# A new emission list for the first layer of a fused delta-rule and two-MLP kernel, without the idle products behind its first block

## The chip, the cores and the metric

The kernel runs on one core of a Trainium2 chip. Its time is device microseconds of one execution; the kernel before was run three times. The engines are TensorE (PE in the profile, with PEld for its weight loads), VectorE (DVE), ScalarE (ACT), GpSimd (POOL) and SyncE (SP), which issues nearly all DMAs.

## What is computed

Three layers follow one another on 4 batches x 768 positions = 3072 tokens of 8 heads x 48 = 384 values: a delta-rule recurrence, an MLP with squared ReLU (384 to 2048 to 384), and a gated MLP (384 to 1536 to 384).

```python
k_n = k / (np.linalg.norm(k, axis=-1, keepdims=True) + 1e-06)
for t in range(S):
    y[:, :, t] = np.einsum('bhd,bhde->bhe', q[:, :, t], state)
    v_old = np.einsum('bhde,bhd->bhe', state, kt)
    state = state + bt[:, :, :, None] * np.einsum('bhd,bhe->bhde', kt, vt - v_old)
...
h = np.maximum(x @ w_in, 0.0);  x = h * h @ w_out
...
gate = 1.0 / (1.0 + np.exp(-(x @ w_gate)));  out = (gate * (x @ w_val)) @ w_out
```

## The kernel before

**Pieces.** The 768 positions are cut into 12 chunks of 64, two chunks (st 0 and 1) to a group, six groups (g 0 to 5) of 512 tokens. The recurrence becomes matrix algebra in a chunk: scores of the keys with themselves, the inverse of a triangular 64x64 matrix per head, then products that carry a state from chunk to chunk. The MLPs run in fp32 accuracy from rounded pairs: each product is three, high x high, low x high, high x low. All of it, up to the middle of the sixth group's MLP, is emitted by one hand-written list of tokens, `ORDER` (lines 28 to 80); line 760 to 762 walk it, and each token calls a small function that issues a few instructions. The instructions of an engine run in the order in which the list issues them, and SP issues its DMAs in that order too, one after the other: a DMA that waits for its buffer holds up those behind it.

The tokens, with the lines of their instructions:

- Loads: `kn`, `kt`, `kc`, `q`, `v`, `k2`, `kz`, `be` (chunks of keys, queries, values, beta), `f,n` (raw weights of MLP block n, 768 KB, L128).
- Weights of MLP block n = 0 to 15, which arrive as 64-bit floats: `hi` (ACT L134), `b` (DVE L139, L143), `b2` (DVE L148, L152), `lo` (POOL L159), `ch` (ACT L204, the rounded half), `cl` (POOL L208, the rest), `sl` (the rest goes to DRAM as `w1d`, L211); `li,n` and `lw,n` fetch a block's low half back (L644) before each use.
- Recurrence of a chunk: `sq`, `sm`, `no` (norms), `a` (key scores, PE L352, DVE L356), `p` (query scores, PE L381 or L366, mask on DVE L387 or L372), `ti`, `r,g,i`, `to`, `t1` (the inverse on DVE: transposes in L426 and L428, row steps L437 and L441 or L450 and L457, transposes out L467 and L470), `ja`, `jb`, `jc` (groups 0 and 1 only: joining 16-row inverses, PE L482 to L512, ACT L490 to L517), `n`, `w` (joining 32-row inverses, PE L525 and L540, ACT L531 and L544), `ks` (PE L553, DVE L561 and L565), `t` (PE L571, ACT L576), `s` (the state, PE L583, DVE L592), `y` (PE L605 and L607, ACT L610), `z` (rearranging by DMA, L623 to L629), `x` (rounded pair of the MLP's input, ACT L116, DVE L117).
- First MLP, n = 16 g + block: `h,n` (9 matmuls of 128x512, L666, and three ACT passes L680 to L683), `g,n` (the low half of the activation, DVE L689), `o,n` (9 matmuls, L704). `h,n` needs `x` of both chunks and `li,n`; `o,n` needs `g,n` and `lw,n`.
- `w2,i,k`: conversion of the second MLP's weights, in six steps. `po`: a group's result to DRAM.
- `d,k`: k idle products of 128x512 whose result nobody reads (L740).

```python
def keep_warm(n):
    if po[0] is None:
        if not idle:
            nc.gpsimd.memset(zeros, 0.0)
            idle.append(ps_o.tile([128, GT], F32, tag="o2", name="idle"))
        out, x = idle[0], zeros
    else:
        out, x = h_tile(h_next[0]), w1h[0][:, 0:GT]
    for _ in range(n):
        nc.tensor.matmul(out=out, lhsT=x[:, 0:128], rhs=x, start=True, stop=True)
```

**Buffers.** Two chunks at a time fit for each load (`bufs=2`), three PSUM banks for the recurrence (most pieces take two), two for `h`, two `wt` tiles and one `wl` tile for the weight conversion, three slots each for `li`, `lw`, `gh` and `gl`. A tile is given back behind its last use in the list, and one that is asked for early holds its slot until then.

**After the list** the kernel's own loops emit the rest: blocks 82 to 95 of the first MLP in their natural order, and the second MLP (L868 to L945), which is not touched.

Of the kernel before, what the change touches and what calls it, by code (L numbers as in the profile page):

```python
# [33 lines left out]
x,0,0 hi,4 b2,3 ti,1,3 ti,1,1 li,1 sl,2 lo,3 y,0,1 z,0,1 r,1,0 d,1 ch,3 f,6 cl,3 sl,3 lw,0 lw,1 kc,1,0 kc,1,1
s,0,1 r,1,1 x,0,1 v,1,0 li,2 q,1,0 hi,5 b,4 b2,4 lo,4 q,1,1 r,1,2 k2,1,0 b,5 d,2 h,0 li,3 f,7 g,0 h,1 ch,4 b2,5
r,1,3 cl,4 r,1,4 sl,4 d,6 lo,5 kn,2,0 li,4 hi,6 g,1 h,2 f,8 ch,5 cl,5 b,6 lw,2 b2,6 lo,6 sl,5 to,1 kt,2,1 o,0
h,3 t1,1 f,9 lw,3 ch,6 cl,6 li,5 sl,6 hi,7 kn,2,1 b,7 p,1,0 o,1 b2,7 g,2 hi,8 lo,7 ch,7 f,10 lw,4 li,6 cl,7 h,4
sl,7 g,3 v,1,1 ja,1,0 b,8 o,2 lw,5 sv,1,0 ja,1,1 p,1,1 hi,9 b2,8 lo,8 ch,8 li,7 kt,2,0 jb,1,0 f,11 sq,2,0 sq,2,1
cl,8 hi,10 g,4 h,5 jb,1,1 b,9 jc,1,0 jc,1,1 sm,2,0 sl,8 o,3 b2,9 lo,9 g,5 ch,9 cl,9 sl,9 lw,6 li,8 b,10 b2,10
hi,11 h,6 o,4 lw,7 lo,10 f,12 ch,10 cl,10 h,7 li,9 g,6 n,1,0 b,11 o,5 hi,12 b2,11 lo,11 sl,10 ch,11 sv,1,1  # L40
sm,2,1 f,13 cl,11 n,1,1 ks,1,0 b,12 b2,12 sl,11 lw,8 no,2 g,7 h,8 w,1,0 li,10 hi,13 b,13 lo,12 ch,12 cl,12 b2,13
o,6 w,1,1 d,18 sl,12 t,1,0 lw,9 d,4 a,2,0 g,8 lo,13 h,9 f,14 ch,13 cl,13 a,2,1 ti,2 o,7 ti,2,1 h,10 kz,2,0 lw,10
hi,14 g,9 li,11 sl,13 li,12 k2,1,1 y,1,0 z,1,0 b,14 b2,14 lo,14 ti,2,3 o,8 f,15 p,2,0 h,11 kz,2,1 s,1,0 lw,11
r,2,0 ch,14 d,1 d,1 cl,14 sl,14 g,10 g,11 ks,1,1 li,13 r,2,1 o,9 x,1,0 hi,15 lw,12 b,15 li,14 d,5 t,1,1 b2,15
h,12 y,1,1 z,1,1 kn,3,0 lo,15 ch,15 cl,15 p,2,1 g,12 r,2,2 o,10 lw,13 x,1,1 r,2,3 sl,15 h,13 o,11 kn,3,1 lw,14
li,15 kc,2,1 h,14 r,2,4 g,13 r,2,5 o,12 r,2,6 li,16 lw,15 li,17 g,14 d,12 h,15 v,2,0 r,2,7 o,13 h,16 kc,2,0
lw,16 r,2,8 g,15 li,18 q,2,0 o,14 lw,17 r,2,9 r,2,10 s,1,1 li,19 h,17 sq,3,0 kt,3,1 g,16 o,15 po,0 lw,18 g,17
h,18 to,2 t1,2 o,16 sq,3,1 li,20 lw,19 li,21 h,19 g,18 o,17 lw,20 sm,3,1 h,20 q,2,1 sm,3,0 no,3 kt,3,0 g,19
n,2,0 li,22 v,2,1 k2,2,0 n,2,1 o,18 lw,21 sv,2,0 ks,2,0 g,20 h,21 li,23 w,2,0 a,3,0 o,19 w,2,1 lw,22 a,3,1 li,24
kz,3,0 h,22 o,20 g,21 ti,3 t,2,0 g,22 h,23 li,25 sv,2,1 y,2,0 lw,23 ti,3,1 o,21 z,2,0 lw,24 ti,3,3 h,24 li,26  # L50
k2,2,1 g,23 p,3,0 kz,3,1 r,3,0 s,2,0 o,22 ks,2,1 g,24 lw,25 li,27 h,25 o,23 lw,26 r,3,1 g,25 h,26 r,3,2 li,28
o,24 lw,27 t,2,1 g,26 x,2,0 r,3,3 h,27 li,29 y,2,1 kn,4,0 o,25 p,3,1 h,28 lw,28 r,3,4 g,27 li,30 w2,0,0 z,2,1
o,26 lw,29 r,3,5 s,2,1 g,28 li,31 kc,3,0 w2,0,1 h,29 o,27 kn,4,1 li,32 r,3,6 lw,30 g,29 r,3,7 h,30 w2,0,2 x,2,1
o,28 lw,31 r,3,8 w2,0,3 g,30 h,31 li,33 q,3,0 w2,0,4 o,29 lw,32 r,3,9 g,31 h,32 li,34 o,30 kt,4,1 h,33 r,3,10
w2,1,0 g,32 lw,33 to,3 li,35 o,31 w2,0,5 lw,34 t1,3 sq,4,0 g,33 h,34 w2,1,1 li,36 v,3,0 sq,4,1 o,32 po,1 w2,1,2
lw,35 sm,4,0 kt,4,0 w2,1,3 sm,4,1 h,35 g,34 sv,3,0 li,37 kc,3,1 n,3,0 o,33 ks,3,0 lw,36 h,36 g,35 li,38 w2,1,4
v,3,1 no,4 w2,1,5 n,3,1 w,3,0 o,34 lw,37 g,36 w2,2,0 h,37 li,39 k2,3,0 t,3,0 o,35 w,3,1 a,4,0 lw,38 g,37 h,38
a,4,1 li,40 q,3,1 w2,2,1 kz,4,0 o,36 lw,39 y,3,0 ti,4 h,39 k2,3,1 w2,2,2 li,41 sv,3,1 s,3,0 g,38 z,3,0 ti,4,1
w2,2,3 o,37 p,4,0 ti,4,3 lw,40 kz,4,1 g,39 w2,2,4 h,40 r,4,0 li,42 o,38 ks,3,1 lw,41 w2,2,5 li,43 g,40 o,39
w2,3,0 h,41 r,4,1 t,3,1 g,41 h,42 li,44 r,4,2 kn,5,0 o,40 x,3,0 w2,3,1 y,3,1 g,42 h,43 lw,42 lw,43 li,45 w2,3,2  # L60
r,4,3 z,3,1 o,41 lw,44 r,4,4 g,43 w2,3,3 h,44 li,46 r,4,5 kn,5,1 o,42 lw,45 w2,3,4 g,44 h,45 li,47 g,45 p,4,1
o,43 kc,4,0 w2,3,5 r,4,6 w2,4,0 lw,46 x,3,1 h,46 li,48 r,4,7 o,44 lw,47 s,3,1 w2,4,1 sq,5,0 li,49 h,47 g,46
q,4,0 r,4,8 o,45 h,48 w2,4,2 o,46 lw,48 r,4,9 g,47 li,50 h,49 w2,4,3 r,4,10 to,4 lw,49 kt,5,1 g,48 w2,4,4 li,51
v,4,0 o,47 lw,50 w2,4,5 po,2 sv,4,0 t1,4 li,52 h,50 w2,5,0 sm,5,0 kc,4,1 g,49 o,48 sq,5,1 lw,51 q,4,1 sm,5,1
g,50 h,51 li,53 n,4,0 w2,5,1 o,49 ks,4,0 kt,5,0 lw,52 w2,5,2 h,52 li,54 no,5 g,51 v,4,1 n,4,1 w,4,0 g,52 o,50
lw,53 w2,5,3 a,5,1 h,53 w2,5,4 k2,4,0 li,55 w,4,1 a,5,0 o,51 t,4,0 lw,54 kz,5,0 g,53 w2,5,5 k2,4,1 h,54 li,56
li,57 ti,5 o,52 w2,6,0 y,4,0 lw,55 h,55 sv,4,1 z,4,0 ti,5,1 p,5,0 kz,5,1 ti,5,3 d,4 s,4,0 o,53 lw,56 g,54 w2,6,1
h,56 g,55 li,58 r,5,0 o,54 kc,5,0 lw,57 w2,6,2 r,5,1 ks,4,1 g,56 w2,6,3 li,59 h,57 o,55 lw,58 li,60 t,4,1 w2,6,4
g,57 r,5,2 w2,6,5 o,56 h,58 x,4,0 y,4,1 h,59 g,58 w2,7,0 lw,59 p,5,1 li,61 r,5,3 z,4,1 o,57 lw,60 r,5,4 g,59
li,62 w2,7,1 q,5,0 kc,5,1 h,60 o,58 lw,61 w2,7,2 g,60 li,63 h,61 r,5,5 o,59 lw,62 w2,7,3 x,4,1 r,5,6 g,61 h,62  # L70
li,64 w2,7,4 o,60 r,5,7 lw,63 s,4,1 w2,7,5 g,62 li,65 r,5,8 w2,8,0 h,63 o,61 lw,64 g,63 h,64 li,66 r,5,9 o,62
w2,8,1 h,65 lw,65 r,5,10 g,64 li,67 to,5 w2,8,2 o,63 v,5,0 lw,66 po,3 t1,5 g,65 li,68 h,66 n,5,0 sv,5,0 w2,8,3
ks,5,0 o,64 v,5,1 w2,8,4 lw,67 h,67 g,66 li,69 w,5,0 w2,8,5 n,5,1 o,65 q,5,1 t,5,0 lw,68 w2,9,0 w,5,1 g,67 h,68
li,70 o,66 k2,5,1 k2,5,0 lw,69 w2,9,1 g,68 h,69 o,67 li,71 sv,5,1 y,5,0 w2,9,2 lw,70 g,69 h,70 s,5,0 li,72
w2,9,3 o,68 z,5,0 lw,71 g,70 li,73 w2,9,4 ks,5,1 o,69 w2,9,5 lw,72 h,71 g,71 li,74 w2,10,0 o,70 h,72 lw,73 t,5,1
x,5,0 g,72 h,73 li,75 o,71 w2,10,1 lw,74 y,5,1 g,73 h,74 w2,10,2 li,76 o,72 z,5,1 li,77 lw,75 w2,10,3 h,75 o,73
w2,10,4 lw,76 g,74 h,76 w2,10,5 li,78 o,74 lw,77 w2,11,0 g,75 g,76 h,77 li,79 o,75 x,5,1 lw,78 w2,11,1 g,77 h,78
li,80 o,76 w2,11,2 lw,79 g,78 o,77 li,81 li,82 w2,11,3 w2,11,4 h,79 h,80 lw,80 g,79 o,78 o,79 w2,11,5 lw,81 g,80
# [966 lines left out]
```

## Time and profile before

| what | value |
|---|---|
| device time, median of 3 runs | 1121.29 us (1120.75 to 1122.94) |
| profiled execution, first to last instruction (its span) | 1116.7 us |
| PE busy | 1041.1 us, 93% |
| DVE busy | 584.0 us, 52% |
| ACT busy | 428.8 us, 38% |
| POOL busy | 151.4 us, 14% |
| mean granted TensorE clock | 0.972 |

Of the profiled execution only the span is known; the median of the runs is 4.6 us longer, for what lies around the span. The shares are averages over very different stages: the recurrence of group 0 has nothing beside it that PE could do, the middle mixes recurrence and first MLP, and the last 450 us are the second MLP alone.

### The profile page before, as it was taken

The page shows a single profiled execution, that of the slowest core. Times are in us where ns is not written, and L with a number is a line of the kernel's source. Part 1 is how long each engine was busy: PE and PEld are TensorE (multiplying, and loading weights), DVE is VectorE, ACT ScalarE, POOL GpSimd, SP SyncE. Part 2 cuts the span into 40 slices and gives each one's busy share as a digit, 9 for nine tenths or more (in the row PEclk, how much of TensorE's full clock was granted, in tenths as well). Part 3 has the DMA queues.
Part 4 walks back from the last instruction along what each step waited for, and adds up shares of the span by engine and source line. Part 5 has one row for each costly group of instructions (what it writes and reads, how often), then busy time and mean ns, then how long its engine had stood idle before and what let it go on. Part 6 is the DMA issues. An engine that isn't in the chain of part 4 may idle for free.

```text
span 1116.7 us, 27013 instructions
## 1 busy us (share of the span) xinstructions
PE 1041.1 (93%) x11764; PEld 862.7 (77%) x11770; DVE 584.0 (52%) x1099; ACT 428.8 (38%) x688; POOL 151.4 (14%) x117
## 2 busy tenths in 40 slices
...
PEclk9998689899999999999999999999999999999999
...
GB/s 270 125 82 212 250 146 178 164 194 155 129 187 261 204 175 227 157 176 201 167 155 170 164 207 164 45 9 49 1 29 29 0 57 1 16 41 1 29 1 29
DMA packets 93030, 135.56 MB, mean 121 GB/s; under 512 B 45552, under 2 KB 72304, under 8 KB 92400
## 3 DMA queue, kind: packets, MB, share of 16 engines
...
q8 instruction: 92, 1.51, 0.6%
...
HBM read 108.63 MB, written 20.45 MB: 116 GB/s over the span
## 4 chain that ended last, share of the span: by engine, by line
PE 87%; DVE 5%; issue 3%; DMA 2%; POOL 1%; ACT 1%; SPq 0%; DVEq 0%; POOLq 0%
PE gv L868 26%; PE o L704 18%; PE h L666 17%; PE o L894 11%; PE o L930 2%; PE att L583 2%; PE att L540 1%; PE att L525 1%; PE att L571 1%; PE att L605 1%; DMA w1s<-in_w_dram 1%; PE att L553 1%; PE att L352 1%; PE h L740 1%; DVE tt L441 1%
## 5 line engine op out<-in xcount | busy, mean ns | idle before, releaser
L876 DVE TENSOR_TENSOR p<-sg,gv 128x512 f32<-128x512 f32 x72 | 49.5, 688 | 252.6 <-PE gv L868 252.6
L680 ACT ACTIVATE gg<-h 128x512 f32<-128x512 f32 x96 | 57.4, 598 | 195.6 <-PE h L666 186.1
L868 PE MATMUL gv<-xhi,w2h 128*128 128x512 f32 x432 | 121.5, 389 | 0.0
L868 PE MATMUL gv<-xlo,w2h 128*128 128x512 f32 x432 | 121.4, 389 | 0.0
L868 PE MATMUL gv<-xhi,w2l 128*128 128x512 f32 x432 | 121.4, 389 | 0.0
L704 PE MATMUL o<-gh,il 128*128 128x512 f32 x288 | 115.0, 399 | 0.0
L874 ACT ACTIVATE sg<-gv 128x512 f32<-128x512 f32 x72 | 43.2, 600 | 172.5 <-PE gv L868 172.5
L878 ACT CAST ph<-p 128x512 fp32r<-128x512 f32 x72 | 44.8, 622 | 156.5 <-DVE p L876 156.5
L689 DVE TENSOR_TENSOR gl<-gg,gh 128x512 fp32r<-128x512 f32 x96 | 72.1, 755 | 54.2 <-ACT gg L683 54.0
L868 PEld LDWEIGHTS gv<-xhi,w2l 128*128 128x128 f32 x432 | 81.1, 188 | 17.0
L868 PEld LDWEIGHTS gv<-xlo,w2h 128*128 128x128 f32 x432 | 81.1, 188 | 16.9
L868 PEld LDWEIGHTS gv<-xhi,w2h 128*128 128x128 f32 x432 | 81.0, 188 | 16.2
L704 PE MATMUL o<-gl,w1h 128*128 128x512 f32 x216 | 87.2, 404 | 5.0 <-DVE gl L689 4.9
L704 PE MATMUL o<-gh,w1h 128*128 128x512 f32 x216 | 90.6, 419 | 0.0
L666 PE MATMUL h<-xhi,il 128*128 128x512 f32 x288 | 83.1, 397 | 2.2 <-DMA il<-w1d 2.2
L880 DVE TENSOR_TENSOR pl<-p,ph 128x512 fp32r<-128x512 f32 x72 | 50.7, 704 | 49.5 <-ACT ph L878 49.5
L159 POOL TENSOR_TENSOR y<-raw 128x768 f32<-128x768 f32 (+1 forms) x16 | 27.9, 1743 | 314.4 <-DVE raw L152 248.4
L117 POOL TENSOR_TENSOR xlo<-x2r,xhi 128x512 fp32r<-128x512 f32 x18 | 24.7, 1370 | 336.8 <-ACT xhi L116 336.8
L894 PE MATMUL o<-ph,w2h 128*128 128x512 f32 x180 | 70.0, 389 | 0.0
L894 PE MATMUL o<-ph,w2l 128*128 128x512 f32 x180 | 70.0, 389 | 0.0
L894 PE MATMUL o<-pl,w2h 128*128 128x512 f32 x180 | 70.0, 389 | 0.0
L666 PE MATMUL h<-xhi,w1h 128*128 128x512 f32 x216 | 65.7, 413 | 3.5 <-ACT xhi L116 3.5
...
## 6 DMA issues: line engine op xcount, KB each, us to landing
...
```

Of the source, the lines that this page charges most:

```text
L117: eng.tensor_tensor(out=dst_lo, in0=src, in1=dst_hi.bitcast(F32), op=ALU.subtract)
L159: nc.gpsimd.tensor_tensor(out=t, in0=c["t"], in1=c["raw"][:, :, 0].bitcast(F32), op=ALU.add)
L666: nc.tensor.matmul(out=ps[:, cs], lhsT=w[:, kc * 128:kc * 128 + 128], rhs=x[:, kc, cs], start=(i == 0 and kc == 0), stop=(i == 2 and kc == ...
L680: nc.scalar.activation(out=gg, in_=ps, func=ACTF.Relu)
L689: nc.vector.tensor_tensor(out=gl, in0=gg, in1=gh.bitcast(F32), op=ALU.subtract)
L704: nc.tensor.matmul(out=po[m], lhsT=w[:, cs], rhs=x, start=(f == 0 and i == 0), stop=(f == NF1 - 1 and i == 2),)
L868: nc.tensor.matmul(out=ps, lhsT=w[:, kc * 128:kc * 128 + 128], rhs=x[:, kc, :], start=(i == 0 and kc == 0), stop=(i == 2 and kc == KD - 1),)
L874: nc.scalar.activation(out=sg, in_=pss[0], func=ACTF.Sigmoid)
L876: nc.vector.tensor_tensor(out=p, in0=sg, in1=pss[1], op=ALU.mult)
L878: nc.scalar.copy(out=ph, in_=p)
L880: nc.vector.tensor_tensor(out=pl, in0=p, in1=ph.bitcast(F32), op=ALU.subtract)
L894: nc.tensor.matmul(out=po2[m], lhsT=w[:, m * 128:m * 128 + 128], rhs=x, start=(f == 0 and i == 0), stop=(f == NF2 - 1 and i == 2),)
```

## The change

The whole of `ORDER` is written anew. The tokens are the same, each as often as before, but for `d`: eight tokens with 51 idle products (`d,6`, `d,18`, `d,4`, two `d,1`, `d,5`, `d,12`, `d,4`), all behind the first `h`, are gone; the seven single products ahead of it remain. No function, buffer, shape or line outside the list changes. First lines of the list:

```diff
 ORDER = """
-kn,0,1 kn,0,0 kt,0,1 be kt,0,0 sq,0,1 f,1 q,0,0 v,0,1 sq,0,0 v,0,0 f,0 kc,0,0 sm,0,1 f,2 sm,0,0 no,0 kc,0,1 hi,1
...
+kn,0,0 kn,0,1 sq,0,0 sm,0,0 d,1 be sq,0,1 sm,0,1 kt,0,1 cj q,0,0 no,0 kt,0,0 cs d,1 kn,2,0 kc,0,1 a,0,1 v,0,0
...
```

**DVE in the inverse of group 0** (L437 and L441 are row steps, L139 to L152 weight conversion, L387 a mask of `p`, L467 and L470 the transposes out, L314 a norm's sum). Before, from the middle of the row steps:

```order
L437 TENSOR_TENSOR tmp_111<-xi,tt 128x120
L441 TENSOR_TENSOR tt<-tt,tmp_111 128x2x10x6
L148 TENSOR_SCALAR y<-wt 128x768
L152 SCALAR_TENSOR_TENSOR w1s_142<-w1s_142,y 128x768
L139 TENSOR_SCALAR y<-wt 128x768
L143 SCALAR_TENSOR_TENSOR wt<-wt,y 128x768
L387 TENSOR_TENSOR pm<-att,mask 128x512 x2
L437 TENSOR_TENSOR tmp_111<-xi,tt 128x126
L441 TENSOR_TENSOR tt<-tt,tmp_111 128x2x9x7
```

Now the end of the row steps, which run without a break from the first, and what follows:

```order
L437 TENSOR_TENSOR tmp_111<-xi,tt 128x30
L441 TENSOR_TENSOR tt<-tt,tmp_111 128x2x15
L467 STREAM_TRANSPOSE t_107<-tt 128x32x32
L387 TENSOR_TENSOR pm<-att,mask 128x512 x2
L139 TENSOR_SCALAR y<-wt 128x768
L143 SCALAR_TENSOR_TENSOR wt<-wt,y 128x768
L148 TENSOR_SCALAR y<-wt 128x768
L152 SCALAR_TENSOR_TENSOR w1s_283<-w1s_283,y 128x768
L470 STREAM_TRANSPOSE xi<-tt 128x32x32
L314 TENSOR_REDUCE s_445<-kn 128x16
```

The conversion and one mask stood inside the row steps; now they stand between the two transposes out.

**PE between the inverse of group 0 and its first state update** (the second number is the tile's width, x64 is both chunks, x32 one of them; L498 and L512 count 64 and 32 a chunk). Before:

```order
L498 MATMUL att<-join,xi 32x16 x128
L512 MATMUL att<-xi,join 32x16 x64
L525 MATMUL att<-t_107,am 32x32 x64
L540 MATMUL att<-n,xi 32x32 x64
L571 MATMUL att<-v,t_107 64x48 x32
L740 LDWEIGHTS join
L740 MATMUL idle<-join 128x512
L605 MATMUL att<-pm,u_112 64x64 x32
L583 MATMUL att<-u_112,k_114 64x48 x32
```

Now:

```order
L498 MATMUL att<-join,xi 32x16 x64
L512 MATMUL att<-xi,join 32x16 x32
L525 MATMUL att<-t_107,am 32x32 x32
L381 MATMUL att<-q,kc 64x64 x32
L540 MATMUL att<-n,xi 32x32 x32
L571 MATMUL att<-v,t_107 64x48 x32
L498 MATMUL att<-join,xi 32x16 x64
L352 MATMUL att<-kt 64x64 x32
L525 MATMUL att<-t_107,am 32x32 x32
L352 MATMUL att<-kt 64x64 x32
L512 MATMUL att<-xi,join 32x16 x32
L583 MATMUL att<-u_112,k_114 64x48 x32
```

Chunk 0 is joined and multiplied (L571) before the joining of chunk 1 begins, and group 1's key scores (L352) and chunk 0's query scores (L381) stand in the gaps.

**PE in the recurrence of group 1** (L666 and L704 are the first MLP). Before:

```order
L540 MATMUL att<-n,xi 32x32 x32
L740 MATMUL h<-w1h_90 128x512 x18
L571 MATMUL att<-v,t_107 64x48 x32
L740 MATMUL h<-w1h_90 128x512 x4
L352 MATMUL att<-kt 64x64 x32
L666 MATMUL h<-xhi,w1h_99 128x512 x3
```

Now, at the same product of chunk 0 (L571):

```order
L540 MATMUL att<-n,xi 32x32 x32
L666 MATMUL h<-xhi,w1h_96 128x512 x3
L666 MATMUL h<-xhi,il 128x512 x3
L666 MATMUL h<-xlo,w1h_96 128x512 x3
L571 MATMUL att<-v,t_107 64x48 x32
L704 MATMUL o_1590<-gh,w1h_95 128x512
```

Where 18 and 4 idle products stood, the blocks of the MLP now stand.

## Rows read from the trace of the kernel before

**Rows 1.** The page: busy time by engine; granted clock in 40 slices.

```profile
PE 1041.1 (93%) x11764; PEld 862.7 (77%) x11770; DVE 584.0 (52%) x1099; ACT 428.8 (38%) x688; POOL 151.4 (14%) x117
...
PEclk9998689899999999999999999999999999999999
```

**Rows 2.** Table by stage: start:end, length, busy of PE, PEld, DVE, ACT, POOL; clock, DMA share, GB/s.

```profile
41.00:64.00 23.00, 15.97 (x769) 14.93 (x768) 6.54 (x12) 11.02 (x21) 1.89 (x2) 1.00 0.15 45
64.00:91.70 27.70, 18.89 (x645) 17.19 (x645) 21.65 (x29) 10.76 (x18) 9.62 (x7) 0.88 0.35 103
91.70:105.57 13.87, 10.29 (x34) 6.92 (x34) 13.23 (x23) 5.35 (x8) 4.57 (x3) 0.75 0.99 261
105.57:160.00 54.43, 42.08 (x861) 33.40 (x859) 41.33 (x50) 25.70 (x41) 25.44 (x14) 0.72 0.65 205
160.00:225.51 65.51, 61.58 (x1244) 49.93 (x1244) 53.65 (x94) 30.39 (x49) 22.84 (x14) 0.95 0.61 178
225.51:602.57 377.06, 370.49 (x5566) 303.48 (x5565) 257.74 (x630) 190.02 (x310) 35.10 (x26) 0.99 0.65 183
602.57:1116.70 514.13, 507.33 (x2269) 423.83 (x2267) 158.11 (x207) 147.28 (x231) 33.06 (x22) 1.00 0.16 51
```

**Rows 3.** Timeline of PE (start, length, line, count): landmarks, and the largest idle group.

```profile
43.72 1.36 PE L498 MATMUL att<-join,xi 32*32 32x16 f32 x87
...
64.02 1.96 PE L571 MATMUL att<-v,t 64*64 64x48 f32 x64
...
91.70 0.96 PE L666 MATMUL h<-xhi,w1h 128*128 128x512 f32 x3 [3.54 <-ACT xhi L116]
...
105.57 0.39 PE L704 MATMUL o<-gh,w1h 128*128 128x512 f32 x1
...
172.48 4.37 PE L740 MATMUL h<-w1h 128*128 128x512 f32 x18
...
225.51 0.39 PE L704 MATMUL o<-gh,w1s 128*128 128x512 f32 x1
```

**Rows 4.** Timeline of DVE, inverse of group 0.

```profile
20.42 0.56 DVE L139 TENSOR_SCALAR y<-wt 128x768 uint32<-128x768 uint32 x1 [0.41 <-ACT wt L134]
21.02 0.96 DVE L143 SCALAR_TENSOR_TENSOR wt<-wt,y 128x768 uint32<-128x768 uint32 x1
...
25.14 0.55 DVE L148 TENSOR_SCALAR y<-wt 128x768 uint32<-128x768 uint32 x1
25.73 0.96 DVE L152 SCALAR_TENSOR_TENSOR w1s<-w1s,y 128x768 f32<-128x768 uint32 x1
26.73 0.56 DVE L139 TENSOR_SCALAR y<-wt 128x768 uint32<-128x768 uint32 x1
27.32 2.47 DVE L143 SCALAR_TENSOR_TENSOR wt<-wt,y 128x768 uint32<-128x768 uint32 x1
29.71 1.28 DVE L387 TENSOR_TENSOR pm<-att,mask 128x512 f32<-128x512 f32 x2
...
32.24 0.29 DVE L437 TENSOR_TENSOR tmp<-xi,tt 128x128 f32<-128x128 f32 x1
...
36.88 2.18 DVE L467 STREAM_TRANSPOSE t<-tt 128x1024 f32<-128x1024 f32 x1
38.96 1.88 DVE L470 STREAM_TRANSPOSE xi<-tt 128x1024 f32<-128x1024 f32 x1
```

**Rows 5.** Timeline of POOL: the pass beside the slow L143.

```profile
26.77 2.20 POOL L159 TENSOR_TENSOR wt<-wt,w1s 128x768 f32<-128x768 f32 x1 [7.86 <-DVE w1s L152]
```

**Rows 6.** Timeline of ACT: evacuations behind `jc`, `n` and `w` of one chunk.

```profile
53.85 0.74 ACT L517 COPY xi<-att 32x256 f32<-32x256 f32 x2
...
57.95 1.20 ACT L531 ACTIVATE n<-att 32x512 f32<-32x512 f32 x2 [0.83 <-PE att L525]
...
61.72 1.18 ACT L544 COPY t<-att 32x512 f32<-32x512 f32 x2 [0.38 <-PE att L540]
```

**Rows 7.** Table by stage, as rows 2: the longest stretch at half clock.

```profile
119.90:143.80 23.90, 16.57 (x466) 13.45 (x467) 18.90 (x19) 8.77 (x14) 11.63 (x6) 0.50 0.65 221
```

More of the change, by code (lines that the diff above doesn't have):

```diff
@@ L34 @@
[L34 to L78, printed above, removed]
```

55 lines of the change are left out of this document (50 added, 5 removed).

## The prediction

> **What bounds the kernel now.** Start with the busy times of the page [rows 1]: PE is busy 93% of the span, no other engine more than 52%, so what PE cannot do early it pays at the end. The clock line says where it is not at full speed: the low digits stand in slices 4 to 8 (84 to 223 us). The table by stage then cuts the span at landmarks of the program [rows 2], which the PE timeline gives [rows 3]: the first `t` at 64.0 us, the first `h` at 91.7, the first `o` at 105.6, the thirteenth (`o,12`) at 225.5. From `o,12` on PE is busy 370.5 of 377.1 us, then 507.3 of 514.1, both at clock 0.99 or more: saturated, so a microsecond won before 225.5 arrives whole at the end, and so does every matmul taken out behind it. Ahead of 225.5 there is room: from 105.6 to 225.5 PE idles 12.4 + 3.9 = 16.3 us and its clock is 0.72 and 0.95; from 41.0 to 91.7 it idles 15.8 us; DVE does only 6.5 us of work from 41 to 64 and is busy 95% of the stretch from 91.7 to 105.6. So the case is decided in the first 225 us: first a chain through the recurrence of group 0, then weight conversion on DVE that falls due all at once, behind an idle stretch.
>
> **The start, up to the first `h`.** Inside the row steps of group 0's inverse DVE now does nothing else. Out go three conversion steps and a mask [rows 4]: 1.52 (L139, L143), 1.51 (L148, L152), 3.03 (L139 and the L143 that took 2.47 beside a POOL pass [rows 5]) and 1.28, in all 7.3 us. So the first transpose out (L467) ends at about 31.7 instead of 39.1. Between it and L470 come a mask (1.28) and one conversion pair (3.03): L470 ends at 31.7 + 1.3 + 3.0 + 1.9 = 37.9 instead of 40.8, 2.9 us earlier.
>
> From there to the first `t` (L571) it was 23.2 us, with the joins of both chunks in between: 43.7 to 64.0, 20.3 us [rows 3]. Now only chunk 0 stands in between: half of that, 10.2, and the three evacuations on ACT (0.74, 1.20 and 1.18 [rows 6]) that the other chunk's matmuls used to cover, 3.1. Between 13.3 and the old 23.2 I take 14, near the low end, because a query-score piece fills one of the gaps: `t` starts at 51.9, 12 us earlier.
>
> From `t` to the first `h` it was 27.7 us. The join of chunk 1 now falls in there, another 10.2, its evacuations covered by group 1's key scores: 51.9 + 27.7 + 10.2 = 89.8. DVE must keep up. It did 28.2 us of work from 41.0 to 91.7 [rows 2]; now three and a half more conversion pairs (3.03 each, 10.6) and six more row steps (twelve instructions of 0.29, 3.5) stand ahead of the second `x`: 42.3 us, so 80.2 without any wait. Each extra pair brings two POOL passes, and one beside L143 cost 2.47 - 0.96 = 1.5 us [rows 4] [rows 5]: 0 to 10.5, I take 5, and DVE is at 85, still inside the 90. Bounds for the first `h`: 85 and 97 (80.2 + 10.5 and the 6.1 us that DVE idled from 64 to 91.7). I take 90, against 91.7.
>
> SP's queue: three more raw weight blocks (768 KB each, 2.3 MB, 8.8 us at the 261 GB/s of a full stretch) and the write-backs of their low halves come ahead of the first `h`; they fall into 41 to 91.7, where the DMA share was 0.15 and 0.35 [rows 2], so I cost them at nothing. If that cover went (a load that waits for its buffer holds up the next ones), the 8.8 us would come on top.
>
> First `h` to first `o`: 13.9 us with PE busy 10.3 at clock 0.75 [rows 2]. The conversion that crowded DVE there is partly done; I take 11. The first `o` stands at 101, 4.6 earlier.
>
> **`o,0` to `o,12`.** It was 119.9 us. PE idled 16.3. At half rate (1.2 GHz) it ran 2 x 0.28 x 54.4 = 30.5 us and 2 x 0.05 x 65.5 = 6.6 us, 37.1 in all; in the longest such stretch it was busy 69% [rows 7], so 25.6 us of busy time at half rate, of which 12.8 is loss. 29 idle products of 0.243 us (18 in 4.37 [rows 3]) are 7.0, gone now. What is left is 119.9 - 16.3 - 12.8 - 7.0 = 83.8 us of full-rate work, and the new order has the same twelve blocks there. Its own losses lie between nothing and the old 29.1. I take the rate of the calmer half: from 160 to 225.5, 3.9 us idle and 3.3 at most for half rate, 11%, so 83.8 / 0.89 = 94, rounded to 95. The reason for the low end: blocks 4 to 6 are converted before the first `h`, and whole MLP blocks stand where PE waited for the second group's inverse and joins. `o,12` then starts at 196, 29.5 us earlier.
>
> On the idle products the row comes first: the 18 at 172.5 run in a stretch where PE is busy 94% at clock 0.95 and end directly in real work, so they cost their time. The Trainium skill, "TensorE: Matmul & The Clock Gate", section "Why this matters for your kernels", asks for no idle gaps between bursts of matmuls, as a gap sends the array back to half rate. By that rule the 7.0 us would be a premium, not a waste, and the sum would lose its 7.0 and what half rate adds. The trace speaks against it only in part: the longest half-rate stretch [rows 7] held no idle product at all, before or now.
>
> **Behind `o,12`.** 16 idle products go, 16 x 0.243 = 3.9 us from a saturated engine. Against that, the new list takes some blocks far out of turn (`h,54` before `h,48`), so that a slot of three is held for six blocks. PE idled 6.6 us in this stage [rows 2]; the new order may add between nothing and 15 us, and I take 5, as DVE has 119 us to spare there. Net: 1 us later.
>
> **Sum.** 29.5 - 1 = 28.5 us less than the span of 1116.7: 1088.2. The median of the runs is 4.6 us above that span, so **1093 us**.
>
> **Rivals.** (1) *DVE is late at the start.* It now does 42 us ahead of the second `x` where it did 28, and POOL passes stretch it. Then the first `h` starts at 97, `o,0` at 108, and with 100 us to `o,12` (208) the gain is 17.5 - 1: 1105; with the loads held up too, 1114. For it: L143 at 2.47 [rows 4]; against it: DVE stood idle for 16.5 of the 23 us from 41 to 64. (2) *Nearly gapless.* `h` at 85, 88 us from `o,0` to `o,12`, no new waits behind: 17 us better than the forecast, 1076. (3) *The gain is given back.* From 225 on PE's idle time grows from 6.6 to about 40 us (the forecast has 11.6); 1120 to 1123. Against it: DVE is at 68% there. (4) *Half rate, slower than before.* Without idle products PE's gaps between `o,0` and `o,12` send it to 1.2 GHz for far longer. Every microsecond of work done at half rate costs one more; the forecast's 28.5 are lost once 28.5 us of work more than now forecast run so, a third of the stage's 83.8. At half of it, 42 us, the time would be 1135. [...] Against it: most of the products stood where PE was busy anyway. This is where the Trainium skill's rule on gaps would lead, on the page named above.
>
> **How the numbers follow.** Forecast 0.60 (1084 to 1101), late DVE 0.17 (1101 to 1114), gapless 0.08, given back 0.05, half rate 0.10. A measurement of this kernel can tell about 0.2%, 2.2 us. Faster: 0.60 + 0.17 + 0.08 = 0.85; the same 0.05; slower 0.10. The range leaves out the last two and the outermost of the others: 1075 to 1114.
>
> **What would show it.** Right: the first transpose out ends near 32, the first `t` starts near 52, the first `h` at 85 to 95, `o,12` at 190 to 202, and from there to `o,79` (377.1 us before) it takes 373 to 383. Wrong at the start: the second L117 ends behind 98 with DVE gapless ahead of it. Wrong on the clock: from `o,0` to `o,12` a granted clock under 0.75. Wrong behind it: PE idle more than 15 us after `o,12`. Wrong altogether: `o,12` at 220 or later.

## The result, and the profile after

The changed kernel takes **1103.2 us** (median of 4 runs, 1101.4 to 1106.8) where the kernel before takes 1121.3 beside it (1120.8 to 1122.9): a ratio of 0.9845, 95% interval 0.9812 to 0.9878. Run again on another chip it took 1101.0 against 1126.8, 0.979 (0.977 to 0.981). It is faster, by 18 us in the first comparison; the forecast was 28 us (1093), with 1075 to 1114 as the range. The profiled execution has a span of 1099.7 us against 1116.7.

The page after, to be held against [rows 1]. The work of DVE, ACT and POOL is what it was; PE has 11.6 us less, and of the low digits of the clock in slices 4 to 8 only the first, an 8, is left, though the idle products that might have held it up are gone; a new 8 stands in slice 22 (577 to 605 us):

```profile
PE 1029.5 (94%) x11719; PEld 854.7 (78%) x11719; DVE 583.5 (53%) x1099; ACT 430.0 (39%) x688; POOL 151.6 (14%) x117
...
PEclk9998999999999999999998999999999999999999
```

The table by stage after, cut at its own landmarks (columns as in [rows 2]: start:end, length, busy time of PE, PEld, DVE, ACT, POOL, then clock, DMA share, GB/s): up to the first `t`, to the first `h`, to the first `o`, the stage up to `o,12` in two pieces, then to `o,79`, to `o,95`, and the second MLP:

```profile
41.00:54.00 13.00, 8.99 (x248) 8.41 (x244) 11.43 (x12) 6.93 (x13) 5.47 (x3) 1.00 0.59 145
54.00:100.34 46.34, 30.68 (x960) 28.74 (x961) 37.29 (x61) 19.28 (x32) 17.66 (x11) 0.94 0.58 179
100.34:110.65 10.31, 9.94 (x156) 7.87 (x157) 9.90 (x15) 6.33 (x10) 4.35 (x2) 0.78 0.99 338
110.65:160.00 49.35, 46.12 (x1195) 37.07 (x1197) 42.52 (x52) 31.12 (x52) 22.59 (x11) 1.00 0.65 202
160.00:202.78 42.78, 40.00 (x767) 32.77 (x759) 37.42 (x59) 20.86 (x35) 17.39 (x11) 0.96 0.66 191
202.78:576.19 373.41, 366.02 (x5553) 300.81 (x5550) 251.95 (x635) 187.92 (x306) 32.00 (x24) 0.99 0.66 182
576.19:648.84 72.65, 65.96 (x281) 54.09 (x279) 26.52 (x30) 37.92 (x58) 6.60 (x4) 0.95 0.50 168
648.84:1099.70 450.86, 444.06 (x1990) 371.56 (x1988) 134.56 (x182) 109.73 (x174) 28.45 (x19) 1.00 0.11 32
```

The PE timeline after, at the landmarks of [rows 3] and at the last place where it loses time (start, length, line; in brackets the idle time before the row and what ended it):

```profile
54.00 2.30 PE L571 MATMUL att<-v,t 64*64 64x48 f32 x60 [0.72 <-issue]
...
61.04 0.83 PE L498 MATMUL att<-join,xi 32*32 32x16 f32 x47 [3.32 <-issue]
...
67.67 1.49 PE L525 MATMUL att<-t,am 32*32 32x32 f32 x47 [3.27 <-issue]
...
100.34 1.65 PE L666 MATMUL h<-xhi,w1h 128*128 128x512 f32 x3 [3.48 <-ACT xhi L116]
...
110.65 0.39 PE L704 MATMUL o<-gh,w1h 128*128 128x512 f32 x1
...
202.78 0.50 PE L704 MATMUL o<-gh,w1s 128*128 128x512 f32 x1
...
580.27 0.84 PE L666 MATMUL h<-xhi,w1h 128*128 128x512 f32 x3
587.80 1.65 PE L666 MATMUL h<-xhi,il 128*128 128x512 f32 x3 [6.69 <-DMA il<-w1d]
589.25 1.48 PE L666 MATMUL h<-xlo,w1h 128*128 128x512 f32 x3
590.53 0.63 PE L704 MATMUL o<-gh,w1h 128*128 128x512 f32 x1
```

Put together, with the times of the kernel before and the forecast's:

| landmark | before | forecast | after |
|---|---|---|---|
| first `t` (L571) | 64.0 | 51.9 | 54.0 |
| first `h` (L666) | 91.7 | 90 | 100.3 |
| first `o` (L704) | 105.6 | 101 | 110.7 |
| `o,0` to `o,12` | 119.9 long | 95 long | 92.1 long |
| `o,12` | 225.5 | 196 | 202.8 |
| `o,12` to `o,79` | 377.1 long | (373 to 383) | 373.4 long |
| `o,79` to `o,95` | 63.2 long | not told apart | 72.7 long |
| second MLP, after `o,95` | 450.9 long | unchanged | 450.9 long |

Of the kernel before, [rows 2] has the last two stages in one; they are cut here at `o,95` (665.8 us in its PE timeline). So two things are missing from the forecast: `o,12` comes 6.8 us later than it said, and between `o,79` and `o,95`, a stage of which the forecast said nothing by itself, 9.4 us are lost again. The L666 at 587.80 shows where: 6.69 us of waiting for a DMA, and behind it matmuls at 0.63 us instead of 0.39.

### The profile page after: what moved, and what is told of

The parts are those of the page before. It is cut to its first block, busy times and chain, and to the rows that moved or that the text cites. A ratio compares the mean times of both kernels' runs of the same rounds, so it can differ in the third digit from the quotient of the medians.

```text
span 1099.7 us, 26954 instructions
## 1 busy us (share of the span) xinstructions
PE 1029.5 (94%) x11719; PEld 854.7 (78%) x11719; DVE 583.5 (53%) x1099; ACT 430.0 (39%) x688; POOL 151.6 (14%) x117
## 4 chain that ended last, share of the span: by engine, by line
PE 87%; DVE 6%; issue 3%; DMA 2%; POOL 1%; SPq 0%; ACT 0%; DVEq 0%; POOLq 0%; ACTq 0%
PE gv L868 27%; PE o L704 18%; PE h L666 18%; PE o L894 11%; PE o L930 2%; PE att L583 2%; PE att L605 1%; PE att L525 1%; PE att L352 1%; PE att L540 1%; PE att L553 1%; PE att L571 1%; PE att L607 1%; DMA kn<-in_kn_dram 1%; PE att L366 1%
## 5 line engine op out<-in xcount | busy, mean ns | idle before, releaser
L689 DVE TENSOR_TENSOR gl<-gg,gh 128x512 fp32r<-128x512 f32 x96 | 74.5, 783 | 86.0 <-ACT gg L683 85.8
L704 PE MATMUL o<-gh,il 128*128 128x512 f32 x288 | 114.0, 396 | 0.0
L666 PE MATMUL h<-xhi,il 128*128 128x512 f32 x288 | 83.3, 398 | 6.7 <-DMA il<-w1d 6.7
L704 PE MATMUL o<-gh,w1h 128*128 128x512 f32 x216 | 88.8, 411 | 0.0
L704 PE MATMUL o<-gl,w1h 128*128 128x512 f32 x216 | 85.9, 397 | 2.3 <-DVE gl L689 2.3
L117 POOL TENSOR_TENSOR xlo<-x2r,xhi 128x512 fp32r<-128x512 f32 x18 | 24.7, 1371 | 333.7 <-ACT xhi L116 333.7
L666 PEld LDWEIGHTS h<-xhi,il 128*128 128x128 f32 x288 | 55.1, 192 | 19.0 <-DMA il<-w1d 7.1
```

The lines of the kernel that those rows point to most:

```text
L117: eng.tensor_tensor(out=dst_lo, in0=src, in1=dst_hi.bitcast(F32), op=ALU.subtract)
L666: nc.tensor.matmul(out=ps[:, cs], lhsT=w[:, kc * 128:kc * 128 + 128], rhs=x[:, kc, cs], start=(i == 0 and kc == 0), stop=(i == 2 and kc == ...
L689: nc.vector.tensor_tensor(out=gl, in0=gg, in1=gh.bitcast(F32), op=ALU.subtract)
L704: nc.tensor.matmul(out=po[m], lhsT=w[:, cs], rhs=x, start=(f == 0 and i == 0), stop=(f == NF1 - 1 and i == 2),)
```

## The experiments

All landmarks are from the profile of each run; "before" is the kernel before on the same chip.

| run | time, us | ratio to before (95%) | first `h` | `o,0` | `o,12` | `o,79` | `o,95` |
|---|---|---|---|---|---|---|---|
| changed, again (c_after) | 1101.0 | 0.979 (0.977-0.981) | 100.7 | 114.3 | 204.6 | 574.9 | 648.4 |
| li,82 earlier (e_li82) | 1092.0 | 0.972 (0.968-0.976) | 100.9 | 111.3 | 201.9 | 574.3 | 639.0 |
| the same, again (c_li82) | 1092.6 | 0.971 (0.968-0.973) | 101.3 | 111.8 | 202.9 | 574.3 | 638.0 |
| before without products (e_before_nod) | 1116.3 | 0.993 (0.991-0.996) | 94.2 | 108.3 | 227.9 | 600.9 | 664.2 |
| changed with products (e_after_d) | 1111.5 | 0.989 (0.986-0.993) | 100.4 | 115.6 | 209.3 | 585.6 | 658.6 |
| new start, old rest (s_startA_restB) | 1107.8 | 0.990 (0.987-0.993) | 100.8 | 109.7 | 219.6 | 590.7 | 654.0 |
| old start, new rest (s_startB_restA) | 1121.3 | 1.000 (0.997-1.003) | 94.0 | 136.8 | 225.9 | 596.5 | 668.5 |
| x earlier on ACT and DVE (e_x00) | 1100.9 | 0.980 (0.976-0.983) | 102.5 | 112.7 | 203.1 | 575.7 | 648.2 |
| li,82 and x earlier (e_best1) | 1097.1 | 0.979 (0.976-0.982) | 98.3 | 114.3 | 209.1 | 581.5 | 645.5 |
| li,82 and f,6 (e_best2) | 1091.8 | 0.970 (0.968-0.971) | 100.8 | 113.5 | 204.4 | 574.8 | 639.2 |
| three loads left out (e_noload) | 1104.9 | 0.980 (0.977-0.984) | 100.7 | 111.3 | 202.3 | 573.4 | 645.9 |
| before with more DMA (e_traffic) | 1119.5 (one run) | | 94.5 | 107.7 | 229.8 | 603.2 | 666.5 |

### The end of the list: one fetch in the wrong place of a queue

In the changed list `li,82` is the last token but one, behind the steps of `w2,11`. `li,83` and `li,80` are fetched before it. SP's own rows in the changed kernel (DMA issues in SP's queue) show what that means:

```profile
579.56 1.10 SPq L644 DMA_DIRECT2D il<-w1d  x2
584.47 0.32 SPq L220 DMA_DIRECT2D w2d<-y  x1
584.84 0.94 SPq L644 DMA_DIRECT2D il<-w1d  x2
```

The store at 584.47 (L220, the step `w2,11,5`) waits for its conversion on POOL, which runs from 582.45 to 584.44; the fetch that block 82 needs is issued right behind it, and PE can go on 3 us later. A slot of `il` was free all the while: `h,81`, which had held it, is through on PE at 574.3.

```diff
-o,78 li,83 lw,79 li,80 o,79 po,4 w2,11,1 lw,80 w2,11,2 h,80 w2,11,3 lw,81 w2,11,4 w2,11,5 li,82 g,80
+o,78 li,83 lw,79 li,80 li,82 o,79 po,4 w2,11,1 lw,80 w2,11,2 h,80 w2,11,3 lw,81 w2,11,4 w2,11,5 g,80
```

> The changed list with one token moved: the fetch li,82 stands right behind li,80 instead of being the last but one of the list, behind the six stores of w2,11. Theory (the fetch is late because SP's queue holds it behind the stores of w2,11): the 6.7 us that PE waits for il ahead of h,82, and the half-rate stretch behind it, go; the time falls from 1103.2 by 7 to 9 us to 1094 to 1096, and o,80 comes about 14 us behind o,79 instead of being further off. Rival (PE is held there by the conversion of w2,11 on DVE and POOL, or by something else that ends at the same time): the wait changes its name and the time stays within 2 us of 1103.

The comparison was made twice, the second time with the changed kernel on the same chip:

> The changed kernel once more, on the chip of the next three runs, so that they are compared with it directly. All theories: 1100 to 1105, a ratio to the kernel before of 0.981 to 0.988.

> The changed list with li,82 behind li,80 once more, beside the changed kernel on one chip. Theory (the wait of 6.7 us ahead of h,82 and the half-rate stretch behind it are all that it saves): 8 to 10 us below the changed kernel. Rival (the first comparison, over two chips, was mostly the difference of chips): less than 5 us.

1092.0 and 1092.6: on one chip 8.4 us below the changed kernel's 1101.0, whose ratio of 0.979 is a little under the 0.981 to 0.988 expected. The rival falls. The 14 us that the first text expected between `o,79` and `o,80` were a slip: that is what it takes with the wait (14.3); without it, it takes 6.1. PE in c_li82, at the place where it had waited for 6.69 us (timeline of PE, as above), now has no gap, and stays at 0.39 us a matmul:

```profile
578.35 0.84 PE L666 MATMUL h<-xhi,w1h 128*128 128x512 f32 x3
579.03 0.84 PE L666 MATMUL h<-xhi,il 128*128 128x512 f32 x3
579.71 0.84 PE L666 MATMUL h<-xlo,w1h 128*128 128x512 f32 x3
580.39 0.39 PE L704 MATMUL o<-gh,w1h 128*128 128x512 f32 x1
```

From `o,79` to `o,95` it takes 63.8 us (64.7 in e_li82), near the 63.2 before the change, where the changed kernel took 72.7 and, again, 73.5. So 8 to 10 us of the stage come with the wait: 6.69 of idle time, and 1.5 from work at half rate behind it (granted clock 0.50 from 587.8 to 593.0). The Trainium skill, "TensorE: Matmul & The Clock Gate", section "Why this matters for your kernels", has the rule for the second part (a gap between bursts of matmuls sends the array back to half rate); here the trace agrees, with 0.63 against 0.39 us for the same matmul behind the gap.

### The idle products: taken out of the old order, put back into the new

```diff
-h,1 ch,4 b2,5 r,1,3 cl,4 r,1,4 sl,4 d,6 lo,5
+h,1 ch,4 b2,5 r,1,3 cl,4 r,1,4 sl,4 lo,5
```

and likewise for the other seven tokens, 51 products in all:

> The kernel before without the 51 idle products behind its first h, all else in the old order. Theory (products that stand where PE has other work cost their time): 16 of them behind o,12 give 3.9 us, the 35 ahead give between nothing and 8.5, so 1109 to 1117. Rival (they hold the clock up where PE would idle): PE's clock between o,0 and o,12 falls below 0.72 and 0.95, and the time is 1121 or more.

> The changed list with the 51 idle products put back beside the tokens that they stood by before: 6 behind h,1, 18 ahead of t,1,0, 4 ahead of a,2,1, 2 behind r,2,0, 5 ahead of t,1,1, 12 behind o,12, 4 ahead of s,4,0. Theory (PE is busy there, at full rate): 51 x 0.22 = 11 us more at most, 1107 to 1114. Rival (they raise a clock that gaps lower): 1103 or less. With the run of the kernel before without them this splits the gain into what the removal is worth and what the order is worth.

The old order without them is 0.66% faster (0.4 to 0.9), some 7 us; the new order with them takes 1111.5 instead of 1101 to 1103, 8 to 11 us more. Neither side shows them holding a clock up. The traces, one for each list, tell in part which ones cost. In the old order the stage from `o,0` to `o,12` is 119.6 us long without them, and it was 119.9 with them: the 29 products there filled time in which PE would have waited. Behind `o,12`, up to `o,95`, it takes 436.3 instead of 440.3 us: the 16 products there cost 4.0. Where the other 3 of the 7 us lie is not shown. In the new order `o,12` comes at 209.3 with them and at 202.8 and, in c_after, 204.6 without: with the 35 ahead of it go 4.6 to 6.5 us, and with the 16 behind it 3.3 to 5.6. The stage from `o,0` to `o,12` alone is 93.7 us long with its 29 products, against 92.1 and 90.4: even there most of them fill time in which PE would have waited. The stage from `o,0` to `o,12` by the table of windows, the first of e_before_nod, the second of e_after_d (columns as above; the clock is the first of the last three):

```profile
108.31:227.91 119.60, 98.54 (x2076) 79.02 (x2075) 94.73 (x133) 55.90 (x90) 48.53 (x27) 0.84 0.62 187
```

```profile
115.58:209.28 93.70, 90.72 (x1977) 74.13 (x1975) 76.07 (x106) 50.74 (x84) 37.57 (x22) 1.00 0.61 185
```

In the old order PE idles 21 us of that stage at a clock of 0.84, with 98.5 us of busy time. It is the order that leaves the gaps, and the products had not closed them: with them the same stage also stood at 0.84 (0.72 and 0.95 in [rows 2]).

### Start or rest: which part of the order brings the gain?

Two lists were spliced at the first `h`.

> The changed list up to its first h (without kn,4,0 and sq,4,0), then what is left of the old list in the old order, without the 51 products. It is to be held against the kernel before without them (1116.3). Theory A (the shorter stage from o,0 to o,12 comes from the start: blocks 4 to 6 converted and group 1's inverse begun ahead of the first h): that stage shrinks from 119.6 us to 95 to 102, and the time is 1098 to 1106. Theory B (it comes from the order behind: whole MLP blocks between the pieces of group 1's recurrence): the stage stays above 110 and, with the first h some 6 us later, the time is 1112 to 1120.

> The old list up to its first h, then what is left of the changed list in its order (the late li,82 included). Theory A (the start makes the stage short): the conversions that the old start leaves undone all stand behind the first h on DVE, the stage from o,0 to o,12 is 105 us or longer, and the time is 1109 to 1116. Theory B (the order behind makes it short): the stage is 90 to 97 us behind a first h at 92, and the time is 1092 to 1098, below the changed kernel's 1103.

Both theories fall: neither half is enough. Held against the old order without products, `o,12` moves from 227.9 to 219.6 with the new start alone (8.3 us), to 225.9 with the new rest alone (2.0), and to 202.8 with both (25.1). The old start with the new rest has one wait that tells why (timeline of PE in s_startB_restA):

```profile
100.06 1.48 PE L666 MATMUL h<-xhi,w1h 128*128 128x512 f32 x3
130.38 1.65 PE L666 MATMUL h<-xhi,il 128*128 128x512 f32 x3 [28.85 <-DMA il<-w1d]
```

SP's queue in that run, up to the fetch (L644) that ends the wait:

```profile
117.91 0.33 SPq L128 DMA_DIRECT2D raw<-in_w_dram  x1
122.17 0.33 SPq L211 DMA_DIRECT2D w1d<-wl  x1
...
126.76 0.33 SPq L211 DMA_DIRECT2D w1d<-wl  x1
127.18 0.38 SPq L644 DMA_DIRECT2D il<-w1d  x1
```

The new rest uses block 3 right behind block 0, and behind the old start the fetch of its low half stands in SP's queue behind loads (L128) and write-backs (L211) that wait for conversions not yet done. Once it has landed, the stage from `o,0` to `o,12` takes 89.0 us at clock 1.00, a little less than the 92.1 of the changed kernel. So the dense stage belongs to the new rest; that this rest can begin 26 us earlier (`o,0` at 110.7 instead of 136.8) belongs to the new start.

### What sets the first `h`: loads, PE's fetching, or DVE's queue?

The forecast had the first `h` at 90; it came at 100.3 to 101.3 in every kernel that has the changed list's start. First, the idle times before the L498 at 61.04 and the L525 at 67.67 are named "issue": PE waits for nothing that the profile shows. The kernel before had such waits too, at the same kind of place (its PE timeline):

```profile
47.11 1.90 PE L498 MATMUL att<-join,xi 32*32 32x16 f32 x127 [2.03 <-issue]
51.38 0.72 PE L498 MATMUL att<-join,xi 32*32 32x16 f32 x38 [2.36 <-issue]
...
55.10 1.09 PE L512 MATMUL att<-xi,join 32*32 32x16 f32 x35 [0.66 <-issue]
```

They are shorter there, where the DMA share was 0.15 [rows 2]. Is it the DMA?

```diff
+fns = dict(e=lambda i: nc.sync.dma_start(out=junk[:, i], in_=w1[:, 8 + i].bitcast(U32)),
-sm,1,0 sm,1,1 f,4 w,0,0 no,1
+sm,1,0 sm,1,1 f,4 e,0 e,1 e,2 e,3 e,4 w,0,0 no,1
```

> The kernel before with five extra copies of 768 KB from DRAM to DRAM behind the load f,4, so that the DMA engines are busy from about 46 to 66 us, where they were nearly idle. All products remain, and the result is the same. Theory (PE's idle times named issue, 2.03 and 2.36 us ahead of L498, come from fetching instructions, and a full DMA makes them longer, as the 3.3 us ones of the changed kernel): they grow to 3 us or more, others that were hidden appear, and the first t comes 2 to 6 us later than 64.0. Rival (these idle times belong to the position in the program, whatever the DMA does): they stay at 2.0 to 2.4 us and the first t at 64.

PE in e_traffic (timeline), and the DMA engines in that stretch (table by windows):

```profile
46.84 1.90 PE L498 MATMUL att<-join,xi 32*32 32x16 f32 x127 [1.75 <-issue]
54.67 0.72 PE L498 MATMUL att<-join,xi 32*32 32x16 f32 x38 [5.93 <-issue]
...
61.14 1.03 PE L512 MATMUL att<-xi,join 32*32 32x16 f32 x33 [3.40 <-issue]
```

```profile
50.00:55.00 5.00, 0.33 (x25) 0.33 (x28) 0.00 (x0) 0.00 (x0) 0.00 (x0) 1.00 1.02 384
```

The wait of 2.36 us becomes 5.93 and the one of 0.66 becomes 3.40, with copies that touch no tile of the kernel; the first `t` comes at 69.5 instead of 64.0. The wait ahead of the row at 46.84 is no longer than before (1.75 for 2.03); the copies are issued from 45.38 on. So these idle times depend on the DMA engines, which is shown. That PE waits for its instructions there can be read from the traces as well. The page of each run has a DMA queue of the kind instruction with the same count (here the changed kernel's; packets, MB, share of 16 engines):

```profile
q8 instruction: 92, 1.51, 0.6%
```

That is 16 KB a packet, and 92 packets for 11719 matmuls and as many weight loads: some 255 instructions in each. By the times of these packets in the traces, each of the 84 waits named issue that are longer than 1 us (from 30 to 225 us, in all 14 traces) ends 1.2 to 1.7 us behind the end of such a packet. What the copies put off is its start: PE runs dry at 49.01 in the kernel before, and the packet starts at 49.03; in e_traffic PE runs dry at 48.74, and the packet starts at 52.42.

The Trainium skill, "Runtime: NRT & Kernel Launch", section "Instruction fetch mechanics", says that the sequencer fetches its program in blocks of 256 instructions by a DMA queue of its own, a cost that is mostly hidden. The spacing agrees: the row at 46.84 has 127 matmuls, each with its weight load, between two such waits. "Mostly hidden" doesn't hold here, where matmuls are this small: 127 of them last 1.90 us and the wait takes 1.75 to 5.93.

But the 5.5 us at the first `t` are 2.8 at the first `h` (94.5 against 91.7) and 0.7 at `o,95`. So the opposite test was made in the changed kernel:

```diff
-            c["raw"] = raw()
-            nc.sync.dma_start(
+            c["raw"] = olds[f] = olds[f - 3] if f in (4, 5, 6) else raw()
+            if f not in (4, 5, 6): nc.sync.dma_start(
```

> The changed list, but blocks 4, 5 and 6 of the first MLP's weights are not loaded: their conversions run on what lies in the tiles of blocks 1, 2 and 3, so all instructions of the compute engines stay and 2.3 MB of loads go. Theory (the loads at the start were not free: they slow PE's instruction fetch, and PE is late for DVE): the idle times of 3.3 us ahead of L498 (61 us) and L525 (67 us) fall to 2.0 to 2.4, those at 35 to 49 us shrink little; the first h comes 2 to 4 us earlier than 100.3 and the time falls by 1 to 3 us. Rival (the stalls are the program's own, and the first h is late because DVE's conversion of three more blocks and its row steps are ahead of it): the stalls stay and the first h comes within 1 us of 100.3.

PE in e_noload (timeline), and DVE:

```profile
61.83 0.83 PE L498 MATMUL att<-join,xi 32*32 32x16 f32 x47 [2.51 <-issue]
...
66.82 1.49 PE L525 MATMUL att<-t,am 32*32 32x32 f32 x47 [1.62 <-issue]
...
100.73 1.65 PE L666 MATMUL h<-xhi,w1h 128*128 128x512 f32 x3 [8.18 <-ACT xhi L116]
```

```profile
92.42 0.29 DVE L441 TENSOR_TENSOR tt<-tt,tmp 128x126 f32<-128x126 f32 x1
92.79 2.49 DVE L117 TENSOR_TENSOR xlo<-xr,xhi 128x768 fp32r<-128x768 f32 x1
```

Each theory is half right. The waits shrink as the first said (3.32 to 2.51, 3.27 to 1.62; the four other runs whose list is the same up to there have 3.32 to 4.43 and 2.72 to 3.54), and the first `h` stays where it was, as the second said: PE's idle time ahead of it grows from 3.48 to 8.18. The time says nothing, as the four executions of this run lie between 1098.8 and 1108.1. What holds the first `h` is on DVE. The same place in the changed kernel (timeline of DVE, with the key scores L356 that wait for PE, the row steps of group 1 ahead of the first L117, and its first transpose out, L467, behind the second):

```profile
71.12 1.29 DVE L356 TENSOR_TENSOR am<-att,gm 128x512 f32<-128x512 f32 x2 [2.88 <-PE att L352]
...
93.25 0.29 DVE L441 TENSOR_TENSOR tt<-tt,tmp 128x126 f32<-128x126 f32 x1
93.62 0.96 DVE L117 TENSOR_TENSOR xlo<-xr,xhi 128x768 fp32r<-128x768 f32 x1
94.50 0.28 DVE L437 TENSOR_TENSOR tmp<-xi,tt 128x120 f32<-128x120 f32 x1
...
100.82 0.95 DVE L117 TENSOR_TENSOR xlo<-xr,xhi 128x768 fp32r<-128x768 f32 x1
...
104.91 2.36 DVE L467 STREAM_TRANSPOSE t<-tt 128x1024 f32<-128x1024 f32 x1
```

From the end of the last L356 to the start of the first L117 it takes 21.2 us in all six runs of this list, e_noload among them. So PE's waits do reach DVE: in e_noload this L117 starts at 92.79, in the five others at 93.62 to 94.66. But there it takes 2.49 us instead of 0.96, beside a pass of POOL (L208, from 92.67 to 94.47), and the lead is lost. That the loads cost nothing at the first `h` can't be concluded from this run.

The L117 of chunk 0 frees the buffer (`xr`) into which chunk 1 is rearranged. Chunk 1 has been copied out on ACT at 92.2; its transfers are issued at 94.68, as L117 ends. That suggests moving the `x`:

```diff
-r,1,0 t,0,1 r,1,1 r,1,2 cl,4 hi,6 x,0,0 y,0,1
+r,1,0 t,0,1 x,0,0 r,1,1 r,1,2 cl,4 hi,6 y,0,1
```

The first try (e_x00) put it ahead of `t,0,1`; the second (e_best1) behind it, together with the move of `li,82`.

> The changed list with one token moved: x,0,0 stands right behind r,1,0, ahead of the row steps r,1,1 and r,1,2. Theory (the second rearranging transfer of group 0 waits for the buffer that the first x gives back, and DVE does that x late because of the row steps): the L117 of chunk 0 ends near 92 instead of 94.6, the first h starts 2 to 3 us earlier than 100.3, and since PE has work from there on, the time falls to 1100 to 1102. Rival (the stretch behind the first h is paced by the conversion of weights on DVE, so an earlier first h only waits longer later): the first h moves, o,12 does not, 1103 within 1 us.

> The changed list with li,82 behind li,80, and x,0,0 directly behind t,0,1, so that on ACT the evacuation of t,0,1 keeps its place ahead of the first x, and on DVE the x comes ahead of the row steps r,1,1 and r,1,2. Theory (the second rearranging transfer waits for the buffer of the first x): its issue comes at about 92.5 instead of 94.7, the first h at 98 instead of 100.3, and the time is 1.5 to 2.5 us below that with li,82 alone, 1089 to 1091. Rival (the start of the first h doesn't set the pace behind it): the first h comes at 98 and the time stays within 1 us of 1092.

In e_x00 the `x` on ACT held up the evacuation of `t,0,1` (L576 at 91.3 instead of 86.9), and the first `h` came 2.2 us later than in the changed kernel; the time of 1100.9 is that of c_after, so it lies in the theory's range without the theory's mechanism. In e_best1 the first `h` comes at 98.34, as expected, and the time is 4.5 to 5 us *worse* than with `li,82` alone, measured on other chips (0.979 of the kernel before, against 0.972 and 0.971). Its PE timeline shows a part of the loss:

```profile
98.34 1.65 PE L666 MATMUL h<-xhi,w1h 128*128 128x512 f32 x3 [3.86 <-ACT xhi L116]
...
109.13 1.26 PE L486 MATMUL att<-t,am 32*16 32x16 f32 x128 [3.72 <-DVE t L467]
110.32 1.65 PE L666 MATMUL h<-xhi,w1h 128*128 128x512 f32 x3
```

PE reaches the join of group 1 earlier and waits there for L467 on DVE, 3.72 us, and then runs its next blocks at half rate (1.65 us for three matmuls, which took 0.96 at that place in the changed kernel): `o,12` comes at 209.1. L467 is late for a pass of POOL again: the last row step ahead of it, an L441 of 128x30, takes 1.69 us at 105.07, beside an L208 that starts at 104.88, where it takes 0.19 in the changed kernel. But c_after and e_best2 wait at this place as well, behind the same long L441 (1.75 and 1.72 us for it, 2.07 and 2.57 of waiting), and reach `o,12` at 204.6 and 204.4. The rest of the loss is work at half rate between `o,0` and `o,12` (PE busy 90.3 of 94.8 us at clock 0.92, against 85.7 of 90.4 at 0.98 in c_after), and that the moved `x` is its cause is not shown. The first `h` is not the landmark that the rest hangs on: here it came earlier and nothing was won. DVE's queue is the likelier pace: from 73 us to the end of that L467 it is busy 31.4 of 34.3 us in the changed kernel.

Last, the load `f,6`, whose block is used only at 87 us, was moved out of the full stretch, with `li,82` at its new place:

```diff
-f,4 v,1,0 f,6 ch,3 cl,3
+f,4 v,1,0 ch,3 cl,3
...
-ks,0,1 ti,1,3 sl,3 y,0,0
+ks,0,1 ti,1,3 sl,3 f,6 y,0,0
```

> The changed list with li,82 behind li,80, and the load f,6 moved from behind f,4 to behind sl,3 (its block is not touched on ACT before 87 us), so that 768 KB less pass in the stretch from 55 to 66 us and arrive in the quiet one behind 73. Theory (PE's instruction fetch is slowed by a full DMA): the idle time named issue ahead of L525, 3.0 to 3.3 us, falls to 2.0 to 2.7; DVE's waits for the key scores behind it shrink by as much; the first h comes 0.5 to 1.5 us earlier and the time is 0 to 2 us below that with li,82 alone. Rival (position alone decides): L525's idle time stays at 3 us or more, same time.

The wait ahead of L525 is 2.72 us, but it is 2.72 to 3.54 in the runs that load `f,6` at its old place, and the wait ahead of L498 is 4.42, at the long end of theirs. The first `h` stands at 100.8, and there is no difference in the time (1091.8 and 1092.6): the theory is not borne out. This and e_li82 are the versions that beat both kernels, by 2.8 to 3.1% against the kernel before.

## Why the prediction was right or wrong

**The sum.** Forecast 28.5 us less in the span, measured 17.0. The 11.5 us between them are 6.8 at `o,12` and 4.8 behind it (446.1 us from `o,12` to `o,95` instead of 440.3 [rows 2], where the forecast allowed a net 1 us). The 4.6 us between span and median were not only what lies around the span: in the executions on record with both numbers that is some 1.8 us, which leaves some 2.8 for the distance of the profiled execution from the median.

**Up to the first `t`: right.** L467 was to end at 31.7 and L470 at 37.9; they end at 31.5 and 37.6. The first `t` came at 54.0 instead of 51.9, behind waits of 0.7 to 2.5 us named issue.

**The first `h`: the step that failed.** The text took the later of two sums, PE's 89.8 and DVE's 85. PE's own came out 8.4 us longer: from the first `t` to the first `h` it took 46.3 us instead of 37.9. PE is busy 30.7 of them, and 8.5 are waits named issue, of which the two stretches that the sum was put together from held some 3.4 (0.4, and half of 5.9). DVE's own sum was nearly right: it is busy 50.2 us from 41.0 to the end of the second L117, where 42.3 and 5 for POOL's passes had been reckoned. But it is idle for another 10.6 us in there, 5.1 of them waiting for PE's key scores (L352) behind the joins. And PE then waits for a hand-over that stands in neither sum: the first `h` starts 5.8 us behind the end of the first L117, over the buffer `xr`, the transfers and the L116 of chunk 1, and before the second L117 ends. Two engines that wait for each other in turn need more than the longer of their sums; the bounds of 85 and 97 held only the sums and 6.1 us of idle time. The three loads, which the text cost at nothing, lengthened PE's waits as e_noload shows (0.8 and 1.7 us) and put off the first L117 by 0.8 us; what they cost at the first `h` is hidden by POOL's passes there.

**`o,0` to `o,12`: the work right, the products' share not.** The 83.8 us of full-rate work show as 84.1 to 84.8 us of PE's busy time in the five runs of this rest that were at clock 1.00 there; 95 was forecast for the stage and 92.1 measured. It began 9.7 us late, though, so `o,12` is 6.8 late. The 29 products there had been costed at 7.0. Taken out of the old order alone they give nothing in this stage, and put back into the new one they lengthen it by 1.6 to 3.4 us. So 7.0 is their work and not what their removal gives: the order closed gaps that they had filled.

**Behind `o,12`: the size near, the place wrong.** The 16 products were put at 3.9 and measure 4.0 in the old order (3.3 to 5.6 in the new one). New waits were allowed 5 us, for blocks held out of turn. From `o,12` to `o,79`, where those blocks stand, there are none: 373.4 us, 3.7 less than before, the products' worth. The loss is one fetch behind the stores of `w2,11` at the list's end, 8 to 9 us in the time. The text spoke of slots; the queue that it had itself described, SP's, was the cause. Without it the time is 1092, where 1093 was forecast; but that is two errors that cancel, an `o,12` 5.9 us late and 4.2 us of allowed waits that did not come (437.1 us from `o,12` to `o,95` in e_li82, against 440.3 + 1).

**Rivals.** The measured 1103.2 lies outside the forecast's own 1084 to 1101, in the 1101 to 1114 of late DVE; that it lies in 1075 to 1114 is owed to the width of that range. Of the signs, the first transpose out, the first `t` and the stage from `o,12` to `o,79` came, and the first `h` and `o,12` missed their windows. Half rate fell: the clock from `o,0` to `o,12` went up, to 1.00 and 0.96. Late DVE is nearest: it had the first `h` at 97 and a time of 1105. It had DVE gapless, which it isn't, and `o,12` at 208, which came at 202.8; that its time is so near is luck, as the late `li,82`, which it did not have, makes up the difference. Gain given back: PE's idle time behind `o,12` went to 14 us, not 40.
